# Turning the output with VectorE block transposes in place of a TensorE transpose, at the end of a decode kernel

## The chip, the cores and the metric

The kernel runs on one core of one Trainium2 chip. The metric is the device time of one execution in microseconds (us). A run is called slow when it is over 1.5% above the fastest run of the same kernel.

## The reference

Two tokens (B = 2, one position each, D = 512) go through a layer norm, then through two branches whose results are added to x: attention over a cache of 8192 positions with 32 heads of 128, and a two-layer ReLU MLP of width 1792. Cut to what matters:

```
xn  = layernorm(A_x)                                   # [2, 1, 512]
q   = xn @ wq                                          # 32 heads of 128
o   = softmax(q . k_cache / sqrt(128)) . v_cache       # caches [2, 32, 8192, 128] bf16
out = A_x + o.reshape(2, 1, 4096) @ wo + relu(xn @ w1) @ w2    # [2, 1, 512] bf16: 2 KB
```

## The kernel before

Each of the five engines (TensorE, VectorE, ScalarE, GpSimd and SyncE, which the profile calls SP) has its own program in this kernel; semaphores tie them together. SP issues nearly all copies; GpSimd waits for the store at the end. 32 steps stream 4 MB of keys and 4 MB of values each. The end is what the change touches. TensorE makes the output with its 512 columns on partitions: `fin` holds four chunks of 128 columns, and in each the two tokens side by side. To store it by rows, it has to be turned.

```python
    yT  = sb([P, Bsz, KT], bf16, "yT")            # 128 partitions x 8
    osb = sb([Bsz * KT, P], bf16, "osb")          # 8 partitions x 128
    fin = ot[0][:, 0:KT * Bsz].rearrange("p (b c) -> p c b", c=KT)      # PSUM, fp32
    ...                                           # SP: loads, then the store
        sp.wait_ge(sE, 1)
        sp.dma_start(
            out.rearrange("b s (c p) -> (b s c) p", p=P), osb[:]        # 8 rows of 256 B
        ).then_inc(dO, 16)
    ...                                           # GpSimd: the last thing it does
        g.wait_ge(dO, 16).then_inc(sG, 1)
    ...                                           # TensorE
        for c in range(NC):
            pe.wait_ge(dW[c], 16)                 # piece c of wo has landed
            ...                                   # fin += wo columns x OX
        t.then_inc(sH, 1)
        pe.wait_ge(sV, 106)
        pe.transpose(
            tp[1][0:Bsz * KT, 0, :], yT[:].rearrange("p b c -> p (b c)"), identb[:]
        ).then_inc(sH, 1)
    ...                                           # VectorE
        v.wait_ge(sH, 4)
        v.tensor_copy(yT[:], ot[0][:, 0:KT * Bsz].rearrange("p (b c) -> p b c", c=KT)).then_inc(sV, 1)
        v.wait_ge(sH, 5)
        v.tensor_copy(osb[:], tp[1][0:Bsz * KT, 0, :]).then_inc(sE, 1)
```

Of the kernel before, what the change touches and what calls it, by code (L numbers as in the profile page):

```python
# [19 lines left out]
def kernel(  # L20
# [13 lines left out]
    P = 128  # L34
    HP = P // 2
    bf16 = mybir.dt.bfloat16
    f32 = mybir.dt.float32

    Bsz, Sq, D = A_x.shape
    _, H, Sk, Dh = A_k_cache.shape  # L40
    Dff = B_w1.shape[1]
    assert Dh == P and D % P == 0 and Dff % P == 0 and Sk % HP == 0
    KT = D // P
# [5 lines left out]
    DQ = Dh // WJ  # L49
    SLOT = KB * Dh  # L50
    assert KB == NG * EG and NP % R == 0 and Dh % WJ == 0 and P == H * DQ
    assert KT * H * Dh == SLOT
    QG = H * Dh // 512
    QH = 512 // Dh
    Z = (QG - 1) * Bsz
# [5 lines left out]
    def sb(shape, dt, name):  # L61
        return ctx.enter_context(nc.sbuf_tensor(name, shape, dt))

    def ps(shape, dt, name):
        return ctx.enter_context(nc.psum_tensor(name, shape, dt))

    def sem(name):
        return tc.alloc_semaphore(name)
# [10 lines left out]
    identb = sb([P, P], bf16, "identb")  # L79
# [26 lines left out]
    OX = sb([P, WJ, Bsz], bf16, "OX")  # L106
    hT = sb([P, FT, Bsz], bf16, "hT")
    ys = sb([Bsz, D], f32, "ys")
    yT = sb([P, Bsz, KT], bf16, "yT")
    osb = sb([Bsz * KT, P], bf16, "osb")  # L110

    tp = [ps([P, EG, P], bf16, f"tp{i}") for i in range(4)]
    Sc = [ps([P, 512], f32, f"Sc{i}") for i in range(2)]
    ot = [ps([P, 512], f32, f"ot{i}") for i in range(2)]

    def S_of(i):
        return Sc[i][:, 0:2 * KB].rearrange("p (k u) -> p k u", u=2)

    def tr_of(i):
        return Sc[i][0:1, 384:384 + P // 2].bitcast(bf16)  # L120
# [11 lines left out]
    sV, sA, sE = sem("sV"), sem("sA"), sem("sE")  # L132
# [4 lines left out]
    sH, sF, sZ = sem("sH"), sem("sF"), sem("sZ")  # L137
# [19 lines left out]
    def load_k(t):  # L157
        nc.sync.dma_start(ks[t % R][:], K_all[t * P:(t + 1) * P, :]).then_inc(dK[t % R], 16)

    def load_v(t):  # L160
        nc.sync.dma_start(vs[t % R][:], V_all[t * P:(t + 1) * P, :]).then_inc(dV[t % R], 16)
# [5 lines left out]
    @(lambda f: f(nc.sync))  # L167
    def _(sp):
        sp.dma_start(w1_sb, B_w1.rearrange("(p kt) f -> p kt f", kt=KT)).then_inc(dW1, 16)  # L169
        sp.dma_start(w2_sb, B_w2.rearrange("(p j) n -> p j n", j=FT)).then_inc(dW2, 16)  # L170
        load_k(0)
        load_k(1)
        load_v(0)
        for t in range(NP - 2):
            sp.wait_ge(pT[NG - 1], t + 1)
            load_k(t + R)
            sp.wait_ge(sW, t + 1)
            load_v(t + 1)
        sp.wait_ge(sW, NP - 1)
        for i in range(2):  # L180
            sl = slice(i * SLOT // 2, (i + 1) * SLOT // 2)
            sp.dma_start(  # L182
                vs[(NP - 1) % R][:, sl], V_all[(NP - 1) * P:NP * P, sl]
            ).then_inc(dH[i], 16)
        for c in range(NC):
            sl = slice(cuts[c], cuts[c + 1])
            sp.dma_start(wo_sb[:, sl, :], wo_v[:, sl, :]).then_inc(dW[c], 16)  # L187
        sp.wait_ge(sE, 1)
        sp.dma_start(
            out.rearrange("b s (c p) -> (b s c) p", p=P), osb[:]  # L190
        ).then_inc(dO, 16)


# [36 lines left out]
    def _(pe):  # L230
# [162 lines left out]
        for c in range(NC):  # L393
# [8 lines left out]
                        stop=(j == WJ - 1 and k == KT - 1),  # L402
                    )
        t.then_inc(sH, 1)
        pe.wait_ge(sV, 106)
        pe.transpose(
            tp[1][0:Bsz * KT, 0, :], yT[:].rearrange("p b c -> p (b c)"), identb[:]
        ).then_inc(sH, 1)

    def kcopy(eng, e):  # L410
        fn = eng.copy if e in ON_ACT else eng.tensor_copy
        fn(kT[e % 4][:], tp[e % 4][:]).then_inc(kR[e], 1)  # L412


    @(lambda f: f(nc.vector))
    def _(v):
        v.memset(eps_t[:], eps).then_inc(sV, 1)
        v.memset(onesb[:], 1.0)
        v.memset(xz[:], 0.0).then_inc(sZ, 1)
        v.memset(prm[R - 1][:], 0.0).then_inc(sP, 1)  # L420
        v.wait_ge(dX, 16)
        v.bn_stats(out=stats[:], in_=xsb[:]).then_inc(sV, 1)
        v.wait_ge(sV, 2)
        v.bn_aggr(out=mv[:], in_=stats[:]).then_inc(sV, 1)
        v.wait_ge(sA, 1)
        v.reciprocal(out=rinv[:], in_=rstd[:]).then_inc(sV, 1)
        v.wait_ge(sV, 4)

        v.tensor_scalar(
            out=xn[:],  # L430
            in0=xsb[:].rearrange("b (p kt) -> b kt p", kt=KT),
            scalar1=mv[:, 0:1],
            scalar2=rinv[:, 0:1],
            op0=ALU.subtract,
            op1=ALU.mult,
        ).then_inc(sV, 1)
        v.wait_ge(sQ, 1)
        v.wait_ge(sZ, 1)
        v.tensor_copy(xz[:, :, Z:Z + Bsz], tpx).then_inc(sV, 1)
        v.wait_ge(sQ, 2)  # L440

        v.tensor_scalar(  # L442
            out=qs[:], in0=qp, scalar1=inv_sqrt, scalar2=None, op0=ALU.mult
        ).then_inc(sV, 1)
        v.wait_ge(sF, 1)
        v.tensor_scalar(
            out=hT[:], in0=hp, scalar1=0.0, scalar2=None, op0=ALU.max,
        ).then_inc(sF, 1)
        v.wait_ge(sQ, 3)

        v.tensor_copy(
            qb[:].rearrange("p (b g l) -> p l g b", b=Bsz, l=QH),
            tpq.rearrange("p l (g b) -> p l g b", b=Bsz),
        ).then_inc(sV, 93)
        v.wait_ge(sF, 3)
        v.tensor_tensor(out=ys[:], in0=y, in1=xsb[:], op=ALU.add).then_inc(sF, 1)

        def pair(i, n):
            for e in range(NG):
                if e not in ON_ACT:  # L460
                    v.wait_ge(pT[e], n)
                    kcopy(v, e)
            v.wait_ge(sS, n)
            for u in range(2):
                half = slice(u * HP, (u + 1) * HP)
                m = v.tensor_reduce(  # L466
                    out=mcol[i][half, :], in_=S_of(i)[half, :, u], axis=AX.X, op=ALU.max
                )
            m.then_inc(sM, 1)
            v.wait_ge(sT, n)  # L470
            v.tensor_reduce(  # L471
                out=mx[i][:], in_=tr_of(i).rearrange("o (u m) -> o u m", u=2),
                axis=AX.X, op=ALU.max, negate=True,
            ).then_inc(sX, 1)

        reg = nc.alloc_register(mybir.EngineType.DVE, "pairno_v")
        v.reg_mov(reg, 0)
        with v.Fori(0, NP // R):
            for r in range(R):
                v.reg_add(reg, reg, 1)  # L480
                pair(r, reg)

        v.wait_ge(sH, 1)
        v.reciprocal(out=RD[:], in_=Sc[0][:, 0:N]).then_inc(sV, 1)
        v.wait_ge(sV, 101)
        v.wait_ge(sO, NP + 1)
        on = OTn[:].rearrange("p b h -> p (b h)")
        v.tensor_tensor(
            out=on[:, 0:N - 2], in0=OTf[:, 2:N], in1=RD[:, 0:N - 2], op=ALU.mult
        ).then_inc(sV, 1)  # L490
        v.wait_ge(sW, NP + 1)
        v.tensor_tensor(
            out=on[:, N - 2:N], in0=ot[1][:, 0:2], in1=RD[:, N - 2:N], op=ALU.mult
        ).then_inc(sV, 1)
        v.wait_ge(sH, 2)
        v.tensor_copy(Ob[:], tp[0][0:H, 0:Bsz, :]).then_inc(sV, 1)
        v.wait_ge(sH, 3)
        v.tensor_copy(
            OX[:], Sc[1][:, 0:Bsz * WJ].rearrange("p (b j) -> p j b", b=Bsz)
        ).then_inc(sV, 1)  # L500
        v.wait_ge(sH, 4)
        v.tensor_copy(yT[:], ot[0][:, 0:KT * Bsz].rearrange("p (b c) -> p b c", c=KT)).then_inc(sV, 1)
        v.wait_ge(sH, 5)
        v.tensor_copy(osb[:], tp[1][0:Bsz * KT, 0, :]).then_inc(sE, 1)


    @(lambda f: f(nc.scalar))
# [67 lines left out]
```

## Time and profile before

| | before |
|---|---|
| median of the first 3 runs | 660.88 us (660.86 to 661.35) |
| span of the profiled execution | 658.6 us |
| HBM read | 280.5 MB, 426 GB/s over the span |
| from the last cast to the issue of the store | 0.77 us |
| from that issue to the end of the span | 2.57 us |

The last two rows are differences of three times in the trace, which has nanoseconds: the start of the cast (655.308), the start of the issue (656.077) and the end of the span (658.644). The page and the timeline round these to 0.01 or 0.1 us. How the views lead there is in the prediction below, with their lines.

### The profile page before, as it was taken

How to read it: one execution, taken by the hardware profiler on the slowest of the kernel's cores; microseconds unless marked ns; L12 is line 12 of the kernel's file. 1: busy time of each engine (PE TensorE's matmuls, PEld its weight loads, DVE VectorE, ACT ScalarE, POOL GpSimd, SP SyncE). 2: the span in 40 equal slices, each digit the busy share in tenths (PEclk: the TensorE clock that was granted, in tenths of full speed). 3: DMA queues.
4: the chain of work that ended last, by engine and by line, in shares of the span. 5: the costliest groups of instructions: out<-in, count | busy, mean ns of one | idle time of the engine just before them, and what ended most of it. 6: DMA issues, size and time to landing. Idle time of an engine off the chain costs nothing.

```text
span 658.6 us, 26859 instructions
## 1 busy us (share of the span) xinstructions
PE 559.9 (85%) x12737; PEld 535.1 (81%) x12737; DVE 253.2 (38%) x436; ACT 255.8 (39%) x403; POOL 9.0 (1%) x46
## 2 busy tenths in 40 slices
PE   2998799987989878879887887997878997887896
PEld 0488798987879878879887887987878987887895
DVE  1144344442434433334443343443434443333441
ACT  1043444443433434334353434344333444333340
POOL 1000000000000000000000000000000000000000
PEclk9799999998998988999898899898989998898988
DMA  8999999999999999999999999999999999999996
GB/s 365 430 444 418 439 430 429 432 428 442 422 442 424 436 428 432 432 428 444 420 442 428 432 430 430 434 430 442 424 436 428 432 432 428 440 424 442 426 424 281
DMA packets 10542, 280.66 MB, mean 426 GB/s; under 512 B 1186, under 2 KB 1188, under 8 KB 1700
## 3 DMA queue, kind: packets, MB, share of 16 engines
q1 hardware_dynamic: 10528, 280.50, 99.2%
q8 instruction: 9, 0.15, 0.1%
q14 instruction: 1, 0.01, 0.0%
q10 hardware_dynamic: 4, 0.00, 0.0%
HBM read 280.50 MB, written 0.00 MB: 426 GB/s over the span
## 4 chain that ended last, share of the span: by engine, by line
DMA 58%; PE 37%; ACT 2%; issue 1%; SPq 1%; ACTq 0%; DVE 0%
DMA ks<-in_A_k_cache_dram 54%; PE tp L285 21%; PE Sc L292 11%; PE ot L305 4%; DMA w_sb<-in_A_wo_dram 4%; ACT kT L412 2%; ACT L412 1%; SPq L187 0%; PE Sc L340 0%; SPq L182 0%; PE Sc L343 0%; SPq L170 0%; SPq L169 0%; SPq L163 0%; PE ot L397 0%
## 5 line engine op out<-in xcount | busy, mean ns | idle before, releaser
L285 PE MATMUL tp<-identb,ks 128*128 128x128 bf16 x4096 | 323.5, 229 | 68.4 <-DMA ks<-in_A_k_cache_dram 68.4
L412 DVE COPY kT<-tp 128x1024 bf16<-128x1024 bf16 x320 | 219.7, 691 | 324.3 <-PE tp L285 324.2
L285 PEld LDWEIGHTS tp<-identb,ks 128*128 128x128 bf16 x4096 | 254.8, 102 | 72.3 <-DMA ks<-in_A_k_cache_dram 72.2
L412 ACT COPY kT<-tp 128x1024 bf16<-128x1024 bf16 x192 | 194.3, 1012 | 233.4 <-PE tp L285 233.3
L292 PE MATMUL Sc<-q,kT 128*128 128x64 bf16 x4096 | 216.8, 196 | 7.6 <-ACT kT L412 5.7
L292 PEld LDWEIGHTS Sc<-q,kT 128*128 128x128 bf16 x4096 | 178.4, 100 | 11.3 <-ACT kT L412 9.0
L305 PE MATMUL ot<-prm,vs 128*128 128x64 bf16 x4224 | 156.1, 192 | 4.2 <-issue 4.2
L305 PEld LDWEIGHTS ot<-prm,vs 128*128 128x128 bf16 x4224 | 139.0, 97 | 7.0 <-issue 4.4
L525 ACT COPY nm<-Sc 128x2 f32<-128x2 f32 x32 | 5.1, 160 | 118.5 <-PE Sc L343 118.5
L529 ACT ACTIVATE prm<-Sc,nm 64x128 bf16<-64x128 f32 x64 | 25.7, 401 | 4.3
L466 DVE TENSOR_REDUCE mcol<-Sc 64x1 bf16<-64x128 f32 x64 | 18.6, 290 | 18.7 <-PE Sc L292 18.3
L412 ACT ACT_TABLE_LOAD x16 | 20.5, 1283 | 2.2
L240 PE MATMUL ot<-vs,xz 128*16 128x512 bf16 x32 | 9.5, 470 | 8.6 <-DMA vs<-in_A_wq_dram 8.6
L517 ACT COPY OTf<-ot 128x2 f32 x32 | 5.1, 160 | 26.9 <-PE ot L305 26.9
L471 DVE TENSOR_REDUCE mx<-Sc 1x2 bf16<-1x128 bf16 x32 | 8.9, 278 | 16.9 <-PE Sc L340 16.9
L240 PEld LDWEIGHTS ot<-vs,xz 128*16 128x16 bf16 x32 | 3.3, 105 | 14.4 <-issue 12.2
L225 POOL COPY q<-qb 128x2 bf16<-128x2 bf16 x32 | 5.8, 184 | 588.9 <-PE Sc L292 566.1
L529 ACT ACTIVATION_READ_ACCUMULATOR prm<-Sc,nm x64 | 11.8, 185 | 0.0
L442 DVE TENSOR_SCALAR qs<-ot 16x512 bf16<-16x512 f32 x1 | 0.7, 679 | 18.0 <-PE ot L240 18.0
L340 PE MATMUL Sc<-identb,mcol 128*1 128x128 bf16 x32 | 7.0, 217 | 0.0
L270 PE MATMUL Sc<-w_sb,hT 128*2 128x512 bf16 x14 | 5.8, 604 | 0.1
L343 PE MATMUL Sc<-mx,onesb 1*128 1x2 bf16 x32 | 5.5, 172 | 0.0
(56 smaller groups left out, 37.5 us busy)
## 6 DMA issues: line engine op xcount, KB each, us to landing
ks<-in_A_k_cache_dram SPq DMA_DIRECT2D x32, 4096.0 KB, 26.7
vs<-in_A_v_cache_dram SPq DMA_DIRECT2D x31, 4096.0 KB, 31.3
vs<-in_A_wq_dram SPq DMA_DIRECT2D x1, 4096.0 KB, 12.1
vs<-in_A_v_cache_dram SPq DMA_DIRECT2D x2, 2048.0 KB, 19.3
w_sb<-in_B_w_dram SPq DMA_DIRECT2D x2, 1792.0 KB, 17.9
w_sb<-in_A_wo_dram SPq DMA_DIRECT2D x1, 1792.0 KB, 25.4
w_sb<-in_A_wo_dram SPq DMA_DIRECT2D x1, 896.0 KB, 27.1
w_sb<-in_A_wo_dram SPq DMA_DIRECT2D x1, 768.0 KB, 28.5
```

The lines of the kernel that those rows point to most:

```text
L225: g.tensor_copy(q2[t % R][:], qb[:, 2 * t:2 * t + 2]).then_inc(sQ1, 1)
L240: i = pe.matmul(qp, lhsT=xz[:, kt, Z - g * Bsz:Z - g * Bsz + QG * Bsz], rhs=vs[1][:, (kt * QG + g) * 512:(kt * QG + g + 1) * 512], start=( ...
L270: i = pe.matmul(y, lhsT=hT[:, j, :], rhs=w2_sb[:, j, :], start=(j == 0), stop=(j == FT - 1),)
L285: t = pe.transpose(tp[e % 4][:, i, :], ks[r][:, kk * Dh:(kk + 1) * Dh], identb[:])
L292: t = pe.matmul(Sc[r][:, 2 * kk:2 * kk + 2 * REP], lhsT=kT[e % 4][:, i, :], rhs=rep(q2[r][:]), start=True, stop=True,)
L305: t = pe.matmul(ot[r][:, 0:2 * REP], lhsT=vs[r][:, kk * Dh:(kk + 1) * Dh], rhs=rep(prm[r][:, kk, :]), start=(kk == 0), stop=(kk == KB - 1),)
L340: pe.transpose(tr_of(r), mcol[r][:], identb[:]).then_inc(sT, 1)
L343: pe.matmul(bc_of(r), lhsT=onesb[:], rhs=mx[r][:], start=True, stop=True).then_inc(sB, 1)
L412: fn(kT[e % 4][:], tp[e % 4][:]).then_inc(kR[e], 1)
L466: m = v.tensor_reduce(out=mcol[i][half, :], in_=S_of(i)[half, :, u], axis=AX.X, op=ALU.max)
L471: v.tensor_reduce(out=mx[i][:], in_=tr_of(i).rearrange("o (u m) -> o u m", u=2), axis=AX.X, op=ALU.max, negate=True,).then_inc(sX, 1)
L529: x = a.activation(out=prm[i][half, :, u], in_=S_of(i)[half, :, u], func=ACTF.Exp, bias=nm[i][half, u:u + 1], scale=1.0, accum_out=RS[half ...
```

## The change

The intent is to take the round trip over TensorE and PSUM out of the end. VectorE's transpose is used here in blocks of 32x32: in each block of 32 partitions the columns become partitions. The eight results of a partition are therefore spread to every fourth of 32 columns, one transpose of 128x32 turns all four blocks at once, and the results stand in every fourth partition as runs of 32 elements (64 B).

```diff
-    yT = sb([P, Bsz, KT], bf16, "yT")
-    osb = sb([Bsz * KT, P], bf16, "osb")
+    yT = sb([P, 32], bf16, "yT")
+    osb = sb([P, 32], bf16, "osb")
...
         sp.dma_start(
-            out.rearrange("b s (c p) -> (b s c) p", p=P), osb[:]
+            out.rearrange("b s (c k n) -> k (b s c) n", c=KT, n=32), osb[0:P:4, :]
         ).then_inc(dO, 16)
...
-        pe.wait_ge(sV, 106)
-        pe.transpose(
-            tp[1][0:Bsz * KT, 0, :], yT[:].rearrange("p b c -> p (b c)"), identb[:]
-        ).then_inc(sH, 1)
...
+        v.memset(yT[:], 0.0)                      # at the start
...
-        v.tensor_copy(yT[:], ot[0][:, 0:KT * Bsz].rearrange("p (b c) -> p b c", c=KT)).then_inc(sV, 1)
-        v.wait_ge(sH, 5)
-        v.tensor_copy(osb[:], tp[1][0:Bsz * KT, 0, :]).then_inc(sE, 1)
+        v.tensor_copy(yT[:, 0:32:4], ot[0][:, 0:KT * Bsz]).then_inc(sV, 1)
+        v.wait_ge(sV, 106)
+        v.transpose(out=osb[:], in_=yT[:]).then_inc(sE, 1)
```

More of the change, by code (lines that the diff above doesn't have):

```diff
@@ L51 @@
     assert KB == NG * EG and NP % R == 0 and Dh % WJ == 0 and P == H * DQ
-    assert KT * H * Dh == SLOT
+    assert KT * H * Dh == SLOT and 4 * KT * Bsz == 32
     QG = H * Dh // 512
```

## The prediction

> **What bounds the kernel now.** I read four views in this order: the page's slices, the chain of work that ended last, the windows of the last 40 us, and the timeline of the last 4 us. The slices and the chain say what sets the time of the whole program:
>
> ```profile
> DMA  8999999999999999999999999999999999999996
> GB/s 365 430 444 418 439 430 429 432 428 442 422 442 424 436 428 432 432 428 444 420 442 428 432 430 430 434 430 442 424 436 428 432 432 428 440 424 442 426 424 281
> ...
> DMA 58%; PE 37%; ACT 2%; issue 1%; SPq 1%; ACTq 0%; DVE 0%
> ```
>
> The DMA engines are full in every slice but the first and the last, at about 430 GB/s, while 280.5 MB of keys, values and weights come in. VectorE is 0% of the chain, rounded. Nothing that the change touches lies in that stream. What can move is the end, so I cut the span at the points where the end's work begins (columns: busy time of PE, weight loads, VectorE, ScalarE, GpSimd, then clock, DMA share, GB/s):
>
> ```profile
> 620.00:655.31 35.31, 30.41 (x744) 28.98 (x742) 9.50 (x20) 8.53 (x18) 0.00 (x0) 0.92 0.94 396
> 655.31:656.08 0.77, 0.27 (x1) 0.08 (x1) 0.38 (x2) 0.00 (x0) 0.00 (x0) 0.50 0.00 0
> 656.08:658.60 2.52, 0.00 (x0) 0.00 (x0) 0.00 (x0) 0.00 (x0) 0.00 (x0) 0.50 0.02 4
> ```
>
> Up to 655.31 us the loads of wo and their matmuls end the work. Then come 0.77 us in which three instructions follow each other and the DMA moves nothing, and then 2.52 us in which the store goes out and the program closes. The timeline names the three and the store (start, duration, engine, line, operation; in brackets the idle time of that engine and what ended it):
>
> ```profile
> 654.90 0.37 PE L397 MATMUL ot<-OX,w_sb 128*128 128x2 bf16 x8 [0.16 <-DMA w_sb<-in_A_wo_dram]
> ...
> 655.31 0.17 DVE L502 CAST yT<-ot 128x8 bf16<-128x8 f32 x1 [5.19 <-PE ot L397]
> 655.53 0.08 PEld L406 LDWEIGHTS tp<-identb,yT 128*8 128x8 bf16 x1 [0.34 <-DVE yT L502]
> 655.53 0.27 PE L406 MATMUL tp<-identb,yT 128*8 128x128 bf16 x1 [0.26 <-DVE yT L502]
> 655.84 0.21 DVE L504 COPY osb<-tp 8x128 bf16<-8x128 bf16 x1 [0.36 <-PE tp L406]
> 656.08 0.37 SPq L189 DMA_DIRECT2D out_dram<-osb  x1
> ```
>
> Each waits for the one before, so the whole of this is on the path that sets the end. The store's own data moves late and briefly. In the DMA view of 656.5 to 657.3 us (40 columns of 0.02 us):
>
> ```profile
> GB/s 0 0 0 0 0 0 0 0 0 0 0 0 0 0 0 0 0 0 38 52 0 13 0 0 0 0 0 0 0 0 0 0 0 0 0 0 0 0 0 0
> DMA packets 16, 0.00 MB, mean 3 GB/s; under 512 B 16, under 2 KB 16, under 8 KB 16
> ```
>
> The bytes move at 656.86 to 656.94, some 0.4 us after the issue ended at 656.45, and about 1.65 us of span are left afterwards for the receipt, GpSimd's wait on it and the program's closing barriers.
>
> **What the Trainium skill says.** On "VectorE: DVE Perf Modes", section "The three transpose paths", a bf16 transpose of 128x128 takes 311 ns on VectorE, in 32x32 blocks only and into SBUF, and 390 ns on TensorE, into PSUM. The trace has TensorE's at 269 ns for 8 columns of weights and the obligatory copy out of PSUM at 212 ns; no VectorE transpose is in it. On "DMA: Bandwidth & Descriptors", section "Why a DMA increments its semaphore by 16 and not by 1", a copy runs on the largest k up to 16 that divides the slowest dimension (of a size over 1) of both sides, and each such engine ends with a write to the semaphore. The trace agrees for the store before: 8 rows on each side give k = 8, so 8 data writes and 8 semaphore writes, and the view above counts 16 packets, all under 512 B. The same page's section "Specifications" puts the minimum for line rate at 512 B, with read-modify-write below; the store is below it before (256 B) and after (64 B), and no row of this trace prices one against the other.
>
> **The change, part by part.**
> Removed on the path: the TensorE transpose from the end of the cast to its own end (0.04 us of handover plus 0.28) and the PSUM copy (0.02 plus 0.21), then the handover to the queue, which stays. So 0.56 us go (655.48, where the cast ends, to 656.05, where the copy ends).
> Added on the path: one VectorE transpose of 128x32 behind a wait of VectorE on its own semaphore. Such a wait costs 0.03 us in this trace (the reciprocal of 0.56 us at 643.70 is followed by a waiting multiply at 644.29). For the transpose I start at the skill's 311 ns for 128 columns and take off 96 columns at one a cycle of 0.96 GHz (its "VectorE" page's clock), 100 ns: **0.21 us, an estimate**. Small VectorE operations of this trace take 0.17 to 0.22 us, which agrees. The sum is 0.24 us, and the store is ready 0.56 - 0.24 = **0.32 us earlier**. The cast writes its 8 columns with a stride of 4, still 8 elements from PSUM; I leave it at 0.17 us.
> Added off the path: a memset of 128x32 bf16 at the start. A 128x60 uint32 memset there is 0.11 us, so this is under 0.11, and VectorE has 0.82 us idle just afterwards, waiting for x. Cost 0.
> The store changes: 32 pieces of 64 B in place of 8 of 256 B, the same 2 KB. The destination is now a three-level pattern of 4 x 8 x 32 and the source has 32 partitions, stepping by 4. By the rule for k the slowest sizes are 4 and 32, so k = 4: **fewer engines, 8 data writes each, instead of 8 engines with one each**; 32 + 4 = 36 packets. If a small write takes 10 to 20 ns (the 16 before were done in about 0.08 us over all engines, so this is an estimate), seven more in a row on each engine add about 0.1 us. The issue itself may take longer too: the two-level issues of SP take 0.33 to 0.47 us each in the timeline, ScalarE's first 0.56; a three-level one with unequal sides is nowhere in the trace. I choose +0.15 us, with 0 to 0.3 possible.
> Sum: -0.32 + 0.10 + 0.15 = about **-0.07 us**. From 660.88 that is **660.8 us**, a change of 0.01%.
>
> **The rivals.**
> 1. *The store costs nothing more.* For it: the bytes are the same 2 KB, and most of the 2.52 us after the issue is fixed. Against it: half the engines, four times the pieces and another pattern. It would be the full -0.32 us, 660.55.
> 2. *The store gives back more than was gained.* For it: small pieces in series on four engines, a heavier issue, and possibly a slower receipt from HBM for 64 B writes; all three are on the path, with nothing to hide behind. Against it: even 8 writes of 50 ns each are 0.4 us. At +0.3 for the issue and +0.4 for the writes the program is 0.4 us slower, 661.3. This I find nearly as likely as my own sum.
> 3. *The VectorE transpose becomes slow* (say 0.5 us, as a fill-and-drain of blocks): then the engines' gain shrinks from 0.32 to about 0 and the time is 661.1. Against it: the skill's 311 ns for four times the columns.
> 4. *The stream moves.* The change leaves every load, wait and buffer of the loop as it is, and only TensorE loses one instruction, at the end. A shift here would be chance.
>
> None comes near 2%, which is 13.2 us: the whole tail from the cast to the end is 3.3 us, so not even deleting it would be 'faster by over 2%'.
>
> **Range and chances.** The runs of before lie within 0.5 us (660.86 to 661.35). The effect lies in -0.35 to +0.45 us by the rivals. Together: 660.3 to 661.3 us 8 times in 10. Within 2%: 0.98; a hundredth each way for a slower state or an accident of the stream.
>
> **What would show it.** In the timeline of the changed kernel: the cast of about 0.17 us; about 0.03 us later a VectorE transpose of about 0.2 us; then the issue, about 0.45 us after the cast's start in place of 0.77. In the DMA view of the end: 36 packets under 512 B, by k = 4; 48 would mean k = 16 and 40 k = 8. The issue's duration against 0.37 us, and the time from issue to the end of the span against 2.52 us, separate rivals 1 and 2. The start of the cast should stay within half a microsecond of 655.31. The prediction is wrong if the issue-to-end time grows by more than 0.8 us, or if the cast itself moves by more than a microsecond, which would mean that the loop's stream has shifted.

## The result, and the profile after

The changed kernel took 661.22 us (median of 6 runs, 660.99 to 661.38), the kernel before 660.87 us (6 runs, 660.79 to 661.35). The ratio is 1.0003, with a 95% interval of 0.9991 to 1.0016. A ratio here is the mean time of one kernel's fast runs over that of the other's fast runs of the same rounds, so it is not quite the ratio of the medians. The output was correct.

The windows of the changed kernel, cut at the same three events as before (columns as in the prediction):

```profile
655.75:656.20 0.45, 0.00 (x0) 0.00 (x0) 0.39 (x2) 0.00 (x0) 0.00 (x0) 0.50 0.00 0
656.20:659.30 3.10, 0.00 (x0) 0.00 (x0) 0.00 (x0) 0.00 (x0) 0.00 (x0) 0.50 0.02 3
```

From cast to issue is now 0.45 us in place of 0.77, and VectorE is busy for 0.39 of it. But from the issue to the end it is 3.14 us in place of 2.57 (by the nanoseconds of the traces; the windows end at the rounded span). The timeline of the changed kernel shows the first reason:

```profile
655.75 0.18 DVE L500 CAST yT<-ot 128x8 bf16<-128x8 f32 x1 [4.03 <-PE ot L398]
655.96 0.21 DVE L502 STREAM_TRANSPOSE osb<-yT 128x32 bf16<-128x32 bf16 x1
656.20 0.71 SPq L190 DMA_DIRECT2D out_dram<-osb  x1
```

The transpose takes 0.21 us and nothing stands between it and the cast but 0.03 us. The last line is the news: the issue of the store holds SP for **0.71 us, against 0.37** for the same 2 KB before. Then the DMA view of 657.1 to 657.9 us of the changed kernel (40 columns of 0.02 us):

```profile
GB/s 0 0 0 0 0 0 0 0 0 0 0 0 0 0 0 0 0 0 0 0 16 19 26 23 13 6 0 0 0 0 0 0 0 0 0 0 0 0 0 0
DMA packets 36, 0.00 MB, mean 3 GB/s; under 512 B 36, under 2 KB 36, under 8 KB 36
```

There are 36 packets: 32 pieces and 4 writes to the semaphore, so four engines carry the store. They move from 657.51 to 657.63 us, in 0.12 us. Between the end of the issue (656.91) and the first byte lie 0.59 us, where before it was 0.42. So the store lost in three places: the issue (+0.34 us), the time from its end to the first byte (+0.17), and the bytes themselves (+0.05).

One thing in this profile I take for scatter: the cast starts at 655.75 us, where before it started at 655.31. In the second profile of the same kernel, below, it starts at 655.39, and in the nine profiles of this study at 655.31 to 655.75. I therefore compare the tails, from the start of the cast to the end of the span, and check their differences against the medians.

### The profile page after: what moved, and what is told of

Its sections match the earlier page's. It is cut to its first block, busy times and chain, and to the rows that moved or that the text cites. A ratio compares the mean times of both kernels' runs of the same rounds, so it can differ in the third digit from the quotient of the medians.

```text
span 659.3 us, 26858 instructions
## 1 busy us (share of the span) xinstructions
PE 558.5 (85%) x12736; PEld 537.3 (81%) x12736; DVE 253.5 (38%) x437; ACT 255.9 (39%) x403; POOL 9.0 (1%) x46
## 4 chain that ended last, share of the span: by engine, by line
DMA 58%; PE 38%; ACT 2%; issue 1%; SPq 0%; DVE 0%; ACTq 0%
DMA ks<-in_A_k_cache_dram 58%; PE tp L286 21%; PE Sc L293 11%; PE ot L306 4%; ACT kT L409 2%; PE ot L398 1%; ACT L409 0%; PE ot L364 0%; PE Sc L341 0%; PE Sc L344 0%; PE Sc L361 0%; SPq L171 0%; SPq L170 0%; SPq L164 0%; PE Sc L384 0%
## 5 line engine op out<-in xcount | busy, mean ns | idle before, releaser
L286 PEld LDWEIGHTS tp<-identb,ks 128*128 128x128 bf16 x4096 | 257.4, 103 | 75.7 <-DMA ks<-in_A_k_cache_dram 75.7
L344 PEld LDWEIGHTS Sc<-mx,onesb 1*128 1x128 bf16 x32 | 2.9, 90 | 1.7
```

Of the source, the lines that this page charges most:

```text
L286: t = pe.transpose(tp[e % 4][:, i, :], ks[r][:, kk * Dh:(kk + 1) * Dh], identb[:])
L344: pe.matmul(bc_of(r), lhsT=onesb[:], rhs=mx[r][:], start=True, stop=True).then_inc(sB, 1)
```

## The experiments

**What is asked.** 32 pieces of 64 B on four engines are one suspect. Another is in the listing of the built program. The builder sets a mark there, called `ant_dge_precooked`; by its name, such a copy is handed to the issuing queue in a prepared form. The kernel before has that mark on all of its 75 copies. The changed kernel has it on every copy but one, the store. In the builds of these runs, the mark was set for two-level patterns from consecutive partitions (8 rows of 256 B, 8 of 64 B, 32 of 64 B alike). It was missing where the partitions are stepped (here by 4) or the target has three levels; the changed store has both. The mark can also be switched off for one copy.

*Theory A*: the loss of the mark makes the store long. *Theory B*: the pieces, or the fewer engines, do. Later came *rival C*, the three levels of the target, and *rival D*, chance. The table has all runs; "first byte" is counted from the end of the issue, "bytes" is from the first to the last packet, "tail" is from the cast to the end of the span, all in us from the nanoseconds of the traces. The last column is the median against the median of before in the same rounds.

| run | cast to issue | issue | first byte | bytes | issue to end | tail | tail against before | median against before |
|---|---|---|---|---|---|---|---|---|
| before | 0.77 | 0.37 | 0.42 | 0.07 | 2.57 | 3.34 | | |
| after | 0.45 | 0.71 | 0.59 | 0.12 | 3.14 | 3.59 | +0.26 | +0.35 |
| r1_store_unmarked | 0.77 | 0.79 | 0.59 | 0.08 | 3.16 | 3.92 | +0.59 | +0.51 |
| r2_pieces_marked | 0.45 | 0.36 | 0.49 | 0.17 | 2.73 | 3.18 | -0.16 | -0.19 |
| r3_four_blocks | 1.07 | 0.37 | 0.42 | 0.08 | 2.57 | 3.64 | +0.30 | +0.24 |
| r4_levels | 0.77 | 0.79 | 0.59 | 0.09 | 3.16 | 3.93 | +0.59 | +0.43 |
| r5_steps | 0.45 | 0.56 | 0.64 | 0.17 | 3.06 | 3.51 | +0.18 | +0.23 |
| r6_four_stores | 0.44 | (4 issues) | | | 3.29 | 3.73 | +0.40 | +0.42 |
| r7_after_again | 0.45 | 0.71 | 0.59 | 0.12 | 3.14 | 3.59 | +0.25 | +0.20 |

All ratios lie between 0.9997 and 1.0008 and every interval holds 1. The tails carry the argument, and the medians follow them: the two columns at the right agree within 0.16 us in every row.

### r1_store_unmarked: the mark alone

The kernel before, and nothing changed but the mark of its store:

```diff
         sp.wait_ge(sE, 1)
+        nc.dge_precook = False
         sp.dma_start(
             out.rearrange("b s (c p) -> (b s c) p", p=P), osb[:]
         ).then_inc(dO, 16)
+        nc.dge_precook = True
```

> The kernel before, with its own store of 8 rows of 256 B, except that the builder's mark for the prepared form of issue is switched off for this one copy (the store of the changed kernel has lost that mark too, because its source steps over partitions and its target has three levels). Theory A, the lost mark makes the issue long: the issue of the store takes 0.65 to 0.75 us in place of 0.37, and from its start to the end of the span 2.9 to 3.1 us in place of 2.57; the program is 0.3 to 0.5 us slower than before. Theory B, the pieces and the four engines make it long: issue 0.37, 2.57 us to the end, time as before.

The timeline of this run:

```profile
655.54 0.17 DVE L504 CAST yT<-ot 128x8 bf16<-128x8 f32 x1 [5.62 <-PE ot L399]
655.76 0.08 PEld L408 LDWEIGHTS tp<-identb,yT 128*8 128x8 bf16 x1 [0.34 <-DVE yT L504]
655.77 0.27 PE L408 MATMUL tp<-identb,yT 128*8 128x128 bf16 x1 [0.26 <-DVE yT L504]
656.07 0.21 DVE L506 COPY osb<-tp 8x128 bf16<-8x128 bf16 x1 [0.36 <-PE tp L408]
656.31 0.79 SPq L190 DMA_DIRECT2D out_dram<-osb  x1
```

The engines' part is that of the kernel before, to 0.01 us. The issue is 0.79 us and the first byte follows its end after 0.59 us: 0.42 and 0.17 us more than before, together 0.58. The DMA view of 657.4 to 658.2 us has the same 16 packets:

```profile
GB/s 0 0 0 0 0 0 0 0 0 0 0 0 0 0 38 39 14 13 0 0 0 0 0 0 0 0 0 0 0 0 0 0 0 0 0 0 0 0 0 0
DMA packets 16, 0.00 MB, mean 3 GB/s; under 512 B 16, under 2 KB 16, under 8 KB 16
```

The time is 661.41 us (661.28 to 661.53) against 660.90 (660.73 to 661.07); the two ranges don't overlap. Theory A stands: the mark alone costs as much as the changed store lost (0.58 us from the issue's start to the end), with 8 pieces on 8 engines. Issue, issue to end and time all lie a little above what I expected of it (0.75, 3.1 and +0.5 us at most). What is open: in every run the unmarked store is the only copy without the mark and is issued once, so whether a second one would cost as much isn't shown.

### r2_pieces_marked: the pieces, with the mark

The changed kernel, its store taken from 32 consecutive partitions in order. The output is wrong.

```diff
-            out.rearrange("b s (c k n) -> k (b s c) n", c=KT, n=32), osb[0:P:4, :]
+            out.rearrange("b s (q n) -> (b s q) n", n=32), osb[0:32, :]
```

> The changed kernel, but the store takes 32 consecutive partitions and writes them in order, so that it carries the mark again with 32 pieces of 64 B; the output is wrong on purpose. Theory A: issue 0.37 us, 2.55 to 2.65 us from its start to the end of the span, cast to issue 0.45 us as in the changed kernel; 0.2 to 0.35 us faster than before. Theory B (pieces): issue 0.6 us or more and about 3.1 us to the end, no faster than before. With 16 engines the packets should be 32 + 16 = 48.

The timeline of this run, and its DMA view of 656.5 to 657.3 us:

```profile
655.71 0.21 DVE L502 STREAM_TRANSPOSE osb<-yT 128x32 bf16<-128x32 bf16 x1
655.95 0.36 SPq L190 DMA_DIRECT2D out_dram<-osb  x1
```

```profile
GB/s 0 0 0 0 0 0 0 0 0 0 0 0 0 0 0 32 14 3 16 16 10 7 7 0 0 0 0 0 0 0 0 0 0 0 0 0 0 0 0 0
DMA packets 48, 0.00 MB, mean 3 GB/s; under 512 B 48, under 2 KB 48, under 8 KB 48
```

With the mark the issue of 32 pieces of 64 B takes 0.36 us, as that of 8 pieces did (0.37). The pieces aren't free: 48 packets take 0.17 us in place of 0.07, and the first comes 0.07 later, so from issue to end it is 2.73 us, 0.16 over before and a little over what I expected (2.55 to 2.65). The time is 660.71 us against 660.90, just short of the 0.2 us that I expected at least, and the only one of these kernels below before; but its output is wrong. With 32 pieces of 64 B and the mark, VectorE's path would thus give 0.32 us less 0.16.

### r3_four_blocks: a correct version with the mark

Four transposes of 32x32, each into its own columns of partitions 0 to 31, so that the store has the rows of before. The listing is cut: `osb` becomes 32 x 128, the cast packs its eight columns side by side, and the store is the one of before.

```diff
-        v.transpose(out=osb[:], in_=yT[:]).then_inc(sE, 1)
+        for k in range(P // 32):
+            q = slice(32 * k, 32 * (k + 1))
+            t = v.transpose(out=osb[:, q], in_=yT[q, :])
+        t.then_inc(sE, 1)
```

> A correct version that keeps VectorE's transposes and the store of before: four transposes of 32x32, each from its own 32 partitions to columns of partitions 0 to 31, then 8 rows of 256 B with the mark. Both theories: issue 0.37 us and 2.57 us to the end. Open is what four small transposes cost in a row: 0.1 us each gives cast to issue 0.65 us, 0.1 us faster than before; 0.2 us each gives 1.05 us, 0.25 us slower than before.

The timeline of this run:

```profile
655.33 0.17 DVE L500 CAST yT<-ot 128x8 bf16<-128x8 f32 x1 [5.07 <-PE ot L398]
655.53 0.84 DVE L504 STREAM_TRANSPOSE osb<-yT 32x32 bf16<-32x32 bf16 x4
656.40 0.37 SPq L190 DMA_DIRECT2D out_dram<-osb  x1
```

The store is that of before again (0.37 us, 2.57 us to the end). The four transposes take 0.84 us, 0.21 each with the gap to the next (0.20 without): a quarter of the partitions costs nearly as much as all of them (0.21). From cast to issue it is 1.07 us, so this version is slower than before (661.14 against 660.90 us).

### r4_levels: the mark lost by another way

The kernel before with its eight rows in another order, so that the target of the store has three levels.

```diff
-            out.rearrange("b s (c p) -> (b s c) p", p=P), osb[:]
+            out.rearrange("b s (c p) -> c (b s) p", p=P), osb[:]
```

The cast writes `yT` in the order of the new rows, so the output is correct.

> The kernel before with its TensorE transpose, its rows in another order, so that the store has 8 pieces of 256 B from consecutive partitions but a three-level target, no mark, and 4 engines (packets 8 + 4 = 12). Theory A: issue 0.65 to 0.75 us, 2.9 to 3.1 us to the end, 0.3 to 0.5 us slower than before, like the run with the mark alone switched off. Theory B with the pieces as cause: issue below 0.45 us and time as before; with the engines as cause: some 0.1 us more to the end at an issue of 0.37 us.

```profile
655.89 0.21 DVE L504 COPY osb<-tp 8x128 bf16<-8x128 bf16 x1 [0.36 <-PE tp L406]
656.12 0.79 SPq L189 DMA_DIRECT2D out_dram<-osb  x1
```

The issue in its timeline is 0.79 us, as in r1 where the target has two levels. The packets are 12 (8 pieces, 4 engines), and halving the engines adds 0.01 us to the bytes. So neither the third level nor the four engines adds anything that this shows; the lost mark accounts for the difference, as in r1. Issue and issue to end are again just above what I expected.

### r5_steps: the mark lost by the stepping alone

The changed kernel with `osb[0:P:4, :]` as it is, but written in order (two levels, wrong output).

```diff
-            out.rearrange("b s (c k n) -> k (b s c) n", c=KT, n=32), osb[0:P:4, :]
+            out.rearrange("b s (q n) -> (b s q) n", n=32), osb[0:P:4, :]
```

> The changed kernel, its 32 partitions still four apart, but written in order (a two-level target, wrong output on purpose), so that only the stepping of the partitions takes the mark away; 16 engines. Theory A (the mark alone decides the issue, the pieces cost 0.16 us after it, as in the run with marked pieces): issue 0.7 to 0.8 us, 3.15 to 3.35 us from its start to the end of the span, time 0.25 to 0.45 us over before. Rival C, the three levels of the target and not the mark were what cost the changed kernel: issue 0.37 us, 2.75 us to the end, 0.2 us faster than before.

```profile
655.69 0.21 DVE L502 STREAM_TRANSPOSE osb<-yT 128x32 bf16<-128x32 bf16 x1
655.93 0.56 SPq L190 DMA_DIRECT2D out_dram<-osb  x1
```

Rival C falls: with two levels the issue is still longer than with the mark (0.56 against 0.36 us in r2, the same 48 packets), and from issue to end it is 3.06 against 2.73 us. But 0.56 is below the 0.7 to 0.8 that I expected, and so are 3.06 us to the end (3.15 to 3.35) and +0.23 us of time (0.25 to 0.45). So the mark lengthens the issue, but it doesn't set its length alone. The unmarked issues took 0.79 (8 engines, 8 pieces), 0.79 (4, 8), 0.71 (4, 32) and 0.56 (16, 32). What makes the difference among them isn't settled: 8 and 4 engines gave the same, and where 4 became 16 the levels of the target changed too.

### r6_four_stores: one transpose and four marked stores

The changed kernel with `yT` packed into columns 0 to 7, and a store for each block of 32 partitions, two from SP and two from ScalarE; GpSimd waits for all four. The listing is cut; `out_k[k]` is the part of the output that block k holds, `dO[k]` the semaphore of its store.

```diff
-        sp.dma_start(
-            out.rearrange("b s (c k n) -> k (b s c) n", c=KT, n=32), osb[0:P:4, :]
-        ).then_inc(dO, 16)
+        for k in range(2):
+            sp.dma_start(out_k[k], osb[32 * k:32 * k + Bsz * KT, :]).then_inc(dO[k], 16)
...                                        # ScalarE, when it is done
+        for k in range(2, 4):
+            a.dma_start(out_k[k], osb[32 * k:32 * k + Bsz * KT, :]).then_inc(dO[k], 16)
```

> A correct version with one transpose on VectorE and four marked stores, each of 8 consecutive partitions in pieces of 64 B, two issued by SP and two by ScalarE. If the second issue of each queue waits for the first: some 0.35 us more than one marked store, 2.9 us from the first issue to the end of the span, time equal to before within 0.1 us (0.2 slower where ScalarE's issues take 0.56 us each). If their completion overlaps fully: 2.6 us, 0.3 us faster than before.

```profile
655.52 0.21 DVE L505 STREAM_TRANSPOSE osb<-yT 128x32 bf16<-128x32 bf16 x1
655.76 0.72 SPq L193 DMA_DIRECT2D out_dram<-osb  x2
655.77 0.65 ACTq L550 DMA_DIRECT2D out_dram<-osb  x2
```

Neither expectation fits. The issues ran side by side, 0.30 to 0.37 us each, and the last packet was done at 657.07 us. But the span ended 3.29 us after the first issue, 0.4 more than the later of my two figures: GpSimd passed its last wait only at 657.69. In the single stores 0.37 to 0.38 us lay between the last packet and that point, here it is 0.63. The semaphore events of the trace separate it. The last of the four semaphores was full 0.51 us after the last packet, against 0.32 to 0.34 in the single stores; GpSimd was past its waits 0.12 us later, against 0.04. So of the excess 0.16 to 0.18 us are a later completion, and the waits on four semaphores are 0.08. Why the completion came later isn't shown. The output is correct, the time 661.30 us against 660.88.

### r7_after_again: the changed kernel once more

> The changed kernel unaltered, beside the others on the same chip. Theory A: 0.32 us gained before the issue and 0.58 us lost after its start, so 0.2 to 0.35 us slower than before. Rival D, the median of the first runs was chance of the load stream: equal to before within 0.1 us.

Its timeline:

```profile
655.39 0.17 DVE L500 CAST yT<-ot 128x8 bf16<-128x8 f32 x1 [5.17 <-PE ot L398]
655.60 0.21 DVE L502 STREAM_TRANSPOSE osb<-yT 128x32 bf16<-128x32 bf16 x1
655.84 0.71 SPq L190 DMA_DIRECT2D out_dram<-osb  x1
```

It took 661.08 us (660.98 to 661.26) against 660.88 (660.70 to 661.09) of before. The tail has the same terms as in the first profile to within 0.01 us (3.59 us). So I read the +0.35 us of the first medians as the +0.26 of the tail plus scatter. Rival D falls in the trace, where the tail repeats; in the totals (+0.20 us) the ranges still overlap.

No correct version beats the kernel before.

## Why the prediction was right, and which term was mis-sized

- *The bound*: right. The load stream fills the DMA engines in both kernels and only the end moved, by a quarter of a microsecond, so "within 2%" was never in doubt, and 661.22 us lies in the range (660.3 to 661.3), close to its upper end. The range held both signs, so landing in it says nothing for the sum.
- *The engines' part, "0.32 us earlier"*: right, 0.769 to 0.450 us. The transpose was estimated at 0.21 us and took 0.211, the wait on VectorE's own semaphore 0.03. That the estimate took off one cycle for each column left out was a guess that no run here tests, since all transposes had 32 columns.
- *The memset, "cost 0"*: right. It took 0.07 us at 1.20 us, and VectorE's idle time before the first norm instruction went from 0.82 to 0.80 us.
- *The engines of the store, k = 4 and 36 packets*: right.
- *"Seven more in a row on each engine add about 0.1 us"*: the bytes took 0.05 us longer. The reason that I gave for it isn't shown: with two pieces on each of 16 engines (r2) they took longer still, 0.17 us.
- *"I choose +0.15, with 0 to 0.3 possible" for the issue*: **this is the term that was mis-sized**. It was +0.34, outside even my bounds, and the sum had no term at all for the later first byte, +0.17. I looked for the reason of a longer issue in the three-level pattern. r1 shows that neither the pattern nor the pieces are needed: the lost mark gives +0.42 and +0.17 by itself.
- *The sum* came out at -0.07 us; the terms measured are -0.32 + 0.34 + 0.17 + 0.05 + 0.02 (from the last packet to GpSimd's release, not in the sum) = +0.26. The sign was wrong, and rival 2, "the store gives back more than was gained", was the one that happened. It was written down as nearly as likely as the sum. Of its three reasons only the heavier issue came true in size (+0.34, where it named +0.3); the writes, priced at +0.4, took +0.05, and the time after the last packet +0.02. The later first byte was in no rival, so that rival 2's 661.3 us came so near is partly luck.
- *Small slips* in the working, which the sum hardly feels: 656.05 - 655.48 is 0.57 us, not 0.56, and 660.88 - 0.32 is 660.56, not 660.55. The 2.52 us from issue to end were cut at the rounded span (2.57 by the nanoseconds), and the 1.65 us after the last byte are 1.70. One early issue of SP took 0.53 us, above the "0.33 to 0.47": it hides in the line of 1.04 us for two. Small VectorE operations of that trace also took 0.15 and 0.28 us.

## What to carry to other kernels

At the end of a kernel the store is on the path as much as the arithmetic before it, so price the copy of a new layout, not only the engines' work: here 0.32 us were won on the engines and 0.58 lost on a copy of the same 2 KB. Look in the built program whether every copy on such a path still has the mark of the prepared form; a source over consecutive partitions and a two-level target kept it here, stepped partitions or a third level lost it, for 0.3 (r5 against r2) to 0.6 us (r1). And before polishing a tail, compare its length with the whole: these were 3.3 of 661 us.

## What the Trainium skill lacked or had wrong

- "DMA: Bandwidth & Descriptors" has nothing on a prepared form of issue on this chip, or on which patterns keep it. The runs show an issue of 0.36 to 0.37 us with the mark and 0.56 to 0.79 without, and the first byte 0.42 to 0.49 us after the issue's end with it and 0.59 to 0.64 without (single stores).
- The same page, section "Why a DMA increments its semaphore by 16 and not by 1": its rule for the number of engines was right in all five patterns of single stores (16, 36, 48, 12 and again 48 packets). It gives no duration of the issue by the number of engines for this chip; the unmarked issues here took 0.56 us at 16 engines and 0.71 to 0.79 at 4 or 8, not separated from the pieces and the levels.
- The same page, section "Specifications", puts read-modify-write below 512 B. All stores lie below it, so no run shows what it costs. Between two sizes below it the difference was small: 32 pieces of 64 B took 0.12 to 0.17 us from first to last packet, 8 pieces of 256 B 0.07 to 0.09.
- "VectorE: DVE Perf Modes", section "The three transpose paths", gives one size, 128x128 in 311 ns. The runs add 128x32 in 211 to 213 ns and 32x32 in 199 to 203 ns: four times the partitions cost about 10 ns, so blocks on different partitions belong in one instruction. How the time goes with the columns no run shows.
- No page has a number for the end of several small stores in place of one: with four stores on two queues the last semaphore was full 0.51 us after the last packet in place of 0.32 to 0.34, and GpSimd was past its waits 0.12 us later in place of 0.04.
